# First batch of a fused attention and MLP kernel: residual rows transposed by TensorE in f32, scaled on the way out of PSUM; pieces of work placed between the score products; the last output tile in parts

## The chip, the cores and the metric

The kernel runs on one core of one Trainium2 chip. A core has a matrix engine (TensorE, "PE"; its loads of stationary operands are listed apart as "PEld"), a vector engine (VectorE, "DVE"), a scalar engine (ScalarE, "ACT"), a general engine (GpSimd, "POOL") and a queue engine (SyncE, "SP"). DMA transfers are issued from the queues of SP, ACT and POOL and carried by 16 DMA engines. Each engine works through its own list of instructions in the order of the program and waits at an instruction until what it needs is there. The metric is device time in microseconds (us), as the median of several runs.

## The reference

Eight batches of 384 tokens go through grouped-query attention (16 query heads, 4 key and value heads, head size 64) and then through a residual MLP with affine layers of width 1024 and a hidden size of 4096:

```python
scores = scale * np.matmul(q, k.transpose(0, 1, 3, 2))
attn = softmax(scores)
x = np.matmul(attn, v)                      # B, S, H*D = 8, 384, 1024

a1 = alpha1 * x + beta1
tok = np.einsum('ts,bsd->btd', w_tok, a1)
u = x + lam * tok
a2 = alpha2 * u + beta2
ch = np.maximum(a2 @ w_ch1, 0.0) @ w_ch2
out = u + lam * ch
```

(The softmax is written out in the reference; the two lines are shortened here.) The vectors alpha1, beta1, alpha2, beta2 and lam have one entry for each of the 1024 columns. Inputs and output are f32.

## The kernel before, in words

**Two kinds of work.** `main(b)` is the channel part of batch b: 32 tiles of the hidden layer (`h`, L394, eight matmuls each over the eight 128-column groups of `a2T`), each moved out of PSUM by ACT or DVE (L402, L404) into `hT`; then six output tiles `ch` of 128 x 512 (L418, 32 matmuls each), which DVE scales by lam and adds to the residual (L423, L424) and SP writes out (L425). `side(b)` is everything ahead of that for a batch: transposed q and k, scores, exponentials, attention output, token mixing, and the transposed `a2T`. `side(b + 1)` is cut into units, and while `main(b)` issues its matmuls a loop strews the units between them at an even pace. So for batches 1 to 7 the side work lies inside the main loop of the batch before. Only `side(0)` has no main loop to lie in. It runs alone, ahead of everything, and is called the head in this text.

**The head.** Its order is written out by hand. `scores(i)`, i = 0 to 17, makes one tile of 128 x 1024 scores (L202) and ACT takes its exponential (L211); two PSUM buffers hold score tiles. The dictionary `at` says which other pieces follow which score tile. They are:

- `q_transpose`, `k_transpose`: six transposes on PE into PSUM and one copy out (L189, L179).
- `split`: DVE splits rows of vectors (each f32 row into three bf16 rows) in a chain of casts and subtractions (L498 to L505). The result stands in `rows_b`. For beta1 it also fills `H` in eight instructions (L507).
- `spread`: four matmuls (L311) and one copy (L313) lay a vector out on all 128 partitions in `vecs`.
- `wtok_transpose` (three times, copies at L292) and `rows_r` (L299, then L302 and L303 make `R`): the transposed token weights and their row sums.
- `av_piece(p, 0)` and `(p, 1)`, p = 0 to 7: 18 matmuls (L236) for one pair of heads; then three DVE steps: reciprocal (L241), normalised into the residual tile `x` (L242), and times alpha1 times lam into `a1` (L246), which reads `x` and `vecs`.
- `tok(p)`: 12 matmuls (L258, L262), which need `a1`, `R` and `H`; DVE adds the result to `x` (L265) and then makes `a2` as bf16, `x` times alpha2 (L270).
- `a2_transpose(p)`: for p = 0 to 2 a transposing DMA from SP (L274); for p = 3 to 7 three PE transposes of the bf16 tile (L280) and a copy by ACT (L283).
- `h_part`: the first four `h` tiles (L150) group by group, so that they can begin before all eight groups of `a2T` are there. These 32 matmuls end the head.

PSUM is shared by tag: `sc` and `mm` have two buffers, `tp` and `av` one each. A piece that takes `tp` or `av` waits until the one before it on that tag has been copied out.

**The queues.** POOL casts and places v, k and three quarters of q for batch 0 (L513, L478, L98), and its queue issues all weight loads: chunks of `w_ch1` (L126, 512 KB each as bf16, a ring of five buffers, refilled when `main` is done with a chunk) and `w_ch2` (L131; 2 MB of it in the head, the rest in pieces between the chunks). The dictionary `loads` gives places in the list of units of `side(0)` at which batch 1's k, q and v are asked for. `load_q(1)` waits until batch 0's last `q_transpose` has read the buffer.

**In batch 1's units** (`b == 1`), `split` and four `spread` calls lay out the two vectors that the head did not (beta1 times lam, and lam).

Of the kernel before, what the change touches and what calls it, by code (L numbers as in the profile page):

```python
# [12 lines left out]
def kernel(  # L13
# [54 lines left out]
    w2 = const.tile([P, NNT, DM], bf, tag="w2", name="w2")  # L68
    hT = const.tile([P, NNT, S], bf, tag="hT", name="hT")
    vecs = const.tile([P, 4, DM], f32, tag="vecs", name="vecs")  # L70
    g1, al2, h1, lam_t = (vecs[:, i] for i in range(4))
    bias1 = const.tile([P, NNT], f32, tag="bias1", name="bias1")
    a2Ts = [const.tile([P, NDT, S + 16 * (1 - i)], bf, tag=f"a2T{i}", name=f"a2T{i}") for i in range(2)]
    kT = const.tile([P, NST, Hkv, P], bf, tag="kT", name="kT")
# [81 lines left out]
    def side(b):  # L156
# [96 lines left out]
        def tok(p):  # L253
            tag, n = ("mm", 2) if first else ("av", 1) if pe_flip else ("tp", 1)
            ps = psum.tile([P, NST, P], f32, tag=tag, name="tok", bufs=n)
            for tt in range(NST):
                for st in range(NST):
                    nc.tensor.matmul(out=ps[:, tt, :], lhsT=wtokT[:, st, tt * P:(tt + 1) * P],  # L258
                                     rhs=a1s[p][:, st, :], start=(st == 0),
                                     stop=(st == NST - 1 and not first))  # L260
                if first:
                    nc.tensor.matmul(out=ps[:, tt, :], lhsT=R[:, tt * P:(tt + 1) * P],  # L262
                                     rhs=H[:, cols(p)], start=False, stop=True)
            u = x[:, :, cols(p)]
            nc.vector.tensor_tensor(out=u, in0=ps, in1=u, op=ADD)  # L265
            if first:
                a2s[p] = hTf[:, 7296 + p % 5 * S:7296 + (p % 5 + 1) * S].rearrange("p (a d) -> p a d", a=NST)
            else:
                a2s[p] = sb.tile([P, NST, P], bf, tag="a2", name="a2", bufs=3)
            nc.vector.tensor_tensor(out=a2s[p], in0=u, in1=bc(al2, p), op=MUL)  # L270

        def a2_transpose(p):
            if not pe_flip or first and p < NP - 5:
                nc.sync.dma_start_transpose(  # L274
                    out=a2T[:, p, :S].rearrange("p (a s) -> p a s", a=NST),
                    in_=a2s[p].rearrange("p a d -> p (a d)"))
                return
            ps = tp_ps([P, NST, P], "av" if first and p % 2 else "tp")
            for tt in range(NST):
                nc.tensor.matmul(out=ps[:, tt, :], lhsT=a2s[p][:, tt, :], rhs=ident,  # L280
                                 is_transpose=True, start=(tt == 0), stop=(tt == NST - 1),
                                 skip_group_check=True)
            nc.scalar.copy(out=a2T[:, p, :S], in_=ps.rearrange("p a b -> p (a b)"))  # L283
# [19 lines left out]
            nc.vector.scalar_tensor_tensor(out=R[:32], in0=t, scalar=masks[2], in1=ps[:32], op0=MUL, op1=ADD)  # L303


        def spread(ps_, vs, tag, eng="ACT"):
            n = len(ps_)
            ps = psum.tile([P, 4, P], f32, tag=tag, name="vec", bufs=1)
            w = vs[1] - vs[0]
            for i, p in enumerate(ps_):  # L310
                nc.tensor.matmul(out=ps[:, i * w:(i + 1) * w], lhsT=sel[:, p:p + 1].to_broadcast([P, P]),  # L311
                                 rhs=rows_b[:, vs[0] * P:vs[1] * P], start=True, stop=True)
            evac(eng)(out=vecs[:, vs[0]:vs[1], ps_[0] * P:(ps_[-1] + 1) * P].rearrange("p v (n d) -> p n v d", n=n),  # L313
                      in_=ps[:, :n * w].rearrange("p (n v) d -> p n v d", n=n))
# [10 lines left out]
        if not first:  # L325
            if pe_flip:
                add(k_transpose, 0)
                add(q_transpose, 0, 2, "DVE", "av")
                add(k_transpose, 2)
                add(q_transpose, 2, 2, "DVE", "av")  # L330
                if b == 1:
                    add(split, 3, 4)
            for j in range(NP + 4):
                if 1 < j < NP + 2:
                    add(av_piece, j - 2, 0)
# [8 lines left out]
                    add(a2_transpose, j - 4)  # L344
                if b == 1 and j < 2:
                    for p in (4 * j, 4 * j + 2):
                        add(spread, (p, p + 1), (2, 4), "tp")
                elif j < 2:
                    us.extend([lambda: None] * 2)
            return us  # L350
# [1 line left out]
        add(q_transpose, 0, 1, "DVE", "av")  # L352
        add(q_transpose, 1, 1, "DVE", "tp")
        lower, upper = range(NP // 2), range(NP // 2, NP)
        at = {1: [(warmup, 3), (split, 0, 1)], 2: [(warmup, 2)],
              3: [(q_transpose, 2, 2, "DVE", "av"), (spread, lower, (0, 1), "tp"), (split, 1, 3)],
              4: [(wtok_transpose, 0, "av"), (spread, lower, (1, 2), "tp")],
              5: [(wtok_transpose, 1, "av"), (wtok_transpose, 2, "tp"), (rows_r, "av")],
              7: [(q_transpose, 4, 2, "ACT")], 8: [(k_transpose, 2, "ACT"), (spread, upper, (0, 1), "av")],
              10: [(q_transpose, 6, 2, "ACT")], 12: [(spread, upper, (1, 2), "av")]}  # L360
        for i in range(18):
            add(scores, i)
            for f, *a in at.get(i, []):
                add(f, *a)
            for p in range(NP):
                last = (9 * p + 8) // 4
                if i == last + 1:
                    add(av_piece, p, 0)
                    add(av_piece, p, 1)
                if i == last + 4:  # L370
                    add(tok_flip if p < NP - 5 else tok, p)
        add(av_piece, NP - 1, 0)
        add(av_piece, NP - 1, 1)
        for f, *a in ((a2_transpose, 3), (tok, 6), (a2_transpose, 4), (h_part, (0, 1), range(3)), (tok, 7),
                      (a2_transpose, 5), (h_part, (2, 3), range(3)), (h_part, range(4), (3, 4)), (a2_transpose, 6),
                      (h_part, range(4), (5,)), (a2_transpose, 7), (h_part, range(4), (6,)), (h_part, range(4), (7,))):
            add(f, *a)
        return us

# [3 lines left out]
    def main(b):  # L383
# [29 lines left out]
        for dw in range(NDW):  # L413
            cs = slice(dw * 512, (dw + 1) * 512)
            for ms in range(NST):
                ps = psum.tile([P, 512], f32, tag="mm", name="ch", bufs=2)
                for nt in range(NNT):
                    nc.tensor.matmul(out=ps, lhsT=hT[:, nt, ms * P:(ms + 1) * P],  # L418
                                     rhs=w2[:, nt, cs], start=(nt == 0), stop=(nt == NNT - 1))
                    if nt % 4 == 3 and nt < NNT - 1:  # L420
                        yield T_C
                o = sb.tile([P, 512], f32, tag="tmp", name="o", bufs=4)
                nc.vector.tensor_tensor(out=o, in0=ps, in1=lam_t[:, cs], op=MUL)  # L423
                nc.vector.tensor_tensor(out=o, in0=o, in1=x[:, ms, cs], op=ADD)  # L424
                nc.sync.dma_start(out=out[b].rearrange("(p st) d -> p st d", st=NST)[:, ms, cs], in_=o)  # L425
                yield T_C

    t_all = 2 * NNT * T_H + 8 * NST * NDW * T_C
# [2 lines left out]
    with tc.manual_schedule(engines=order):  # L431
# [16 lines left out]
        qst, vst = (stage[:, i:i + Hkv * NST * D].rearrange("p (h st d) -> p h st d", h=Hkv, st=NST)  # L448
                    for i in (0, Hkv * NST * D))
        wtok_in = stage[:, 1536:2112].bitcast(bf).rearrange("p (tt s) -> p tt s", tt=NST)  # L450
        be2 = stage[:, 2112:2112 + NDT]
        R = stage[:, 2120:2312].bitcast(bf)
        H = stage[:, 2312:2824].bitcast(bf)
        ones = stage[:, 2824:2840].bitcast(bf)
        masks = [stage[:32, 2840 + i:2841 + i] for i in range(3)]
        sel4 = stage[:32, 2844:2852]
        sel = stage[:, 2852:2856].bitcast(bf)
        for t in (stage[:, 2120:2824], rows_b, sel):
            nc.vector.memset(t, 0.0)
        nc.sync.dma_start(out=vst, in_=v[0].rearrange("h (p st) d -> p h st d", st=NST))  # L460

        for i, ap in enumerate((moe_alpha1, moe_alpha2, moe_beta1, moe_lam)):
            nc.sync.dma_start(out=rows_f[:, i * P:(i + 1) * P],
                              in_=bass.AP(tensor=ap.tensor, offset=ap.offset, ap=[[0, 4], [P, NP], [1, P]]))
        load_k(0, [2])
        with nc.allow_non_contiguous_dma(reason="one small vector, once"):
            nc.sync.dma_start(out=be2, in_=moe_beta2.rearrange("(dt di) -> di dt", di=P))
        for h in (0, 2):
            nc.scalar.dma_start(out=qst[:, h:h + 2], in_=q[0, h:h + 2].rearrange("h (p st) d -> p h st d", st=NST))
        xs[0] = sb.tile([P, NST, DM], f32, tag="x", name="x", bufs=2)  # L470
# [12 lines left out]
        for t in vt:  # L483
            nc.vector.memset(t[:, :, :, D:], 1.0)
        AX = mybir.AxisListType.X
        for i, m in enumerate(masks):
            nc.vector.tensor_reduce(out=m, in_=ident[:32, 8 * (i + 1):24 + 8 * (i // 2)], op=ADD, axis=AX)
        nc.vector.tensor_scalar(out=masks[2], in0=masks[2], scalar1=-1.0, scalar2=None, op0=MUL)
# [1 line left out]
            for t, n in ((sel, 24), (sel4, 32)):  # L490
                nc.vector.tensor_reduce(out=t[:n], in_=ident[:n, :n].rearrange("p (k c) -> p c k", c=NP), op=ADD, axis=AX)

        def split(lo, hi):
            c = slice(lo * P, hi * P)
            for i in (0, 2):
                if lo <= i < hi:
                    r = rows_f[:, i * P:(i + 1) * P]
                    nc.vector.tensor_tensor(out=r, in0=r, in1=rows_f[:, 3 * P:], op=MUL)  # L498
            src, dst = rows_f, rows_t
            for m in masks[:2]:  # L500
                nc.vector.tensor_copy(out=rows_b[:32, c], in_=src[:, c])
                nc.vector.scalar_tensor_tensor(out=dst[:, c], in0=rows_b[:32, c], scalar=m, in1=src[:, c],
                                               op0=MUL, op1=mybir.AluOpType.subtract)
                src, dst = dst, src
            nc.vector.tensor_copy(out=rows_b[:32, c], in_=src[:, c])  # L505
            for p in range(NP if lo <= 2 < hi else 0):
                nc.vector.tensor_scalar(out=H[:32, p * P:(p + 1) * P], in0=rows_b[:32, 2 * P:3 * P],  # L507
                                        scalar1=sel4[:, p:p + 1], scalar2=None, op0=MUL)

        place_k(0, 0)  # L510
        for h, cp in ((0, nc.vector.tensor_copy), (2, nc.scalar.copy)):
# [81 lines left out]
```

## Time and profile before

| | |
|---|---|
| median of 9 runs | 819.62 us (818.81 to 820.61) |
| time of the profiled execution | 820.61 us |
| span of its profile | 818.7 us |
| PE busy, share of the span | 797.3 us, 97% |
| DVE, ACT, POOL busy | 352.7, 225.9, 184.5 us |
| first matmul of `main(0)` (L394) | 47.75 us |
| last DVE step of the last output tile | ends at 815.70 us |

The profiled execution is the slowest of the nine, 1.0 us over their median. All positions in the text are us from the start of its span. A row of the timeline gives start, duration, engine, line, operation, the tiles written and read, and in brackets how long the engine had been idle before it and what ended the wait. A matmul's duration holds the time that it takes to run through the array, so a row of matmuls that follow each other closely overlaps the next row; the time that one costs PE is read from start to start.

The head in stretches, busy us of each engine and the mean granted clock of PE:

| stretch | PE | DVE | ACT | POOL | clock |
|---|---|---|---|---|---|
| 6 to 10 | 2.81 | 2.88 | 3.01 | 3.58 | 1.00 |
| 10 to 14 | 1.86 | 3.76 | 2.88 | 4.00 | 1.00 |
| 14 to 18 | 1.15 | 3.96 | 1.15 | 4.00 | 0.72 |
| 18 to 22 | 2.05 | 2.38 | 0.42 | 0.17 | 0.50 |
| 22 to 26 | 4.00 | 3.24 | 1.48 | 0.00 | 0.50 |
| 26 to 30 | 3.51 | 2.59 | 3.94 | 0.00 | 1.00 |

### The profile page before, as it was taken

What the parts mean: (1) busy time and instruction counts of PE and PEld (TensorE: products, weight loads), DVE (VectorE), ACT (ScalarE), POOL (GpSimd) and SP (SyncE); (2) the same over time, 40 slices, a digit from 0 to 9 for tenths busy, and PEclk for the clock granted to TensorE, in tenths of its full rate; (3) what the DMA queues carried; (4) which work ended last, traced back from release to release, by engine and by line L of the source; (5) the groups of instructions that cost most, each with busy time, mean ns of one, the idle gap of its engine ahead of it and who ended that gap; (6) DMA issues with size and microseconds to landing.
All of it is one profiled execution on the core that took longest, in us unless ns stands there. A gap on an engine that the chain in (4) does not pass through costs nothing.

```text
span 818.7 us, 13994 instructions
## 1 busy us (share of the span) xinstructions
PE 797.3 (97%) x6020; PEld 447.1 (55%) x6073; DVE 352.7 (43%) x689; ACT 225.9 (28%) x300; POOL 184.5 (23%) x230
## 2 busy tenths in 40 slices
PE   5999999999999999999999999999999999999997
PEld 2665655565555655556555664556545565556543
DVE  7754554254442444334443444524454344442222
ACT  4745321332114321133112331033210432102100
POOL 6234440225002240022401232022500221003000
PEclk8899999999999999999999999999999999999999
DMA  9999999899959991699927999589995998129610
GB/s 167 198 180 200 202 215 171 134 168 174 80 99 180 172 160 46 136 182 170 146 69 136 178 174 103 107 132 176 173 87 99 152 177 125 36 57 193 87 39 38
DMA packets 260589, 112.85 MB, mean 138 GB/s; under 512 B 109744, under 2 KB 254256, under 8 KB 260528
## 3 DMA queue, kind: packets, MB, share of 16 engines
q0 software_dynamic: 197760, 83.28, 90.0%
q1 hardware_dynamic: 62224, 28.30, 14.4%
q8 instruction: 47, 0.77, 0.4%
q10 hardware_dynamic: 544, 0.39, 0.2%
q14 instruction: 14, 0.11, 0.0%
HBM read 170.53 MB, written 12.58 MB: 224 GB/s over the span
## 4 chain that ended last, share of the span: by engine, by line
PE 88%; DVE 2%; issue 1%; ACT 0%; ACTq 0%; DVEq 0%
PE ch L418 40%; PE h L394 37%; PE av L236 4%; PE sc L202 4%; PE tok L258 3%; DVE a1f L249 0%; DVE x L242 0%; DVE a L251 0%; DVE hT L404 0%; PE tp L280 0%; DVE rinv L241 0%; ACT es L211 0%; DVE o L423 0%; DVE o L424 0%; PE tp L186 0%
## 5 line engine op out<-in xcount | busy, mean ns | idle before, releaser
L394 PE MATMUL h<-a2T,w 128*128 128x384 bf16 (+1 forms) x2016 | 349.4, 327 | 1.0 <-ACT hT L402 0.4
L418 PE MATMUL ch<-w,hT 128*128 128x512 bf16 x1483 | 345.6, 380 | 3.4 <-issue 1.0
L394 PEld LDWEIGHTS <-w 128*128 128x128 bf16 x2016 | 189.3, 98 | 125.5 <-issue 9.0
L126 POOL DMA_DIRECT2D w<-in_moe_w_ch_dram x128 | 112.3, 879 | 545.2 <-PE h L394 494.8
L418 PEld LDWEIGHTS <-hT 128*128 128x128 bf16 x1536 | 142.3, 98 | 155.4 <-issue 4.6
L211 ACT ACTIVATE es<-sc 128x1024 bf16<-128x1024 f32 x126 | 123.2, 1021 | 281.9 <-PE sc L202 281.9
L404 DVE TENSOR_SCALAR hT<-h,bias 128x384 bf16<-128x384 f32 x128 | 79.0, 618 | 187.0 <-PE h L394 186.4
L402 ACT ACTIVATE hT<-h,bias 128x384 bf16<-128x384 f32 x128 | 74.2, 580 | 226.0 <-PE h L394 202.3
L423 DVE TENSOR_TENSOR o<-ch,vecs 128x512 f32<-128x512 f32 x48 | 33.0, 688 | 92.7 <-PE ch L418 92.7
L265 DVE TENSOR_TENSOR x<-tok,x 128x384 f32<-128x384 f32 x64 | 35.5, 555 | 77.4 <-PE tok L258 75.8
L236 PEld LDWEIGHTS <-es 128*128 128x128 bf16 x1008 | 45.8, 97 | 21.4 <-ACT es L211 0.9
L236 PE MATMUL av<-v,es 128*128 128x65 bf16 x1008 | 49.2, 193 | 0.8 <-ACT es L211 0.8
L202 PE MATMUL sc<-qT,kT 64*128 64x384 bf16 (+2 forms) x576 | 45.8, 275 | 0.7 <-ACT hT L211 0.3
L258 PEld LDWEIGHTS <-wtokT 128*128 128x128 bf16 x576 | 38.0, 98 | 13.1 <-issue 0.8
L241 DVE RECIPROCAL rinv<-av 128x6 f32<-128x6 f32 x64 | 12.7, 198 | 66.5 <-PE av L236 66.2
L258 PE MATMUL tok<-a,wtokT 128*128 128x128 bf16 x504 | 37.3, 220 | 0.0
L242 DVE TENSOR_TENSOR x<-av,rinv 128x384 f32<-128x384 f32 x64 | 35.7, 558 | 2.3
L202 PEld LDWEIGHTS <-kT 64*128 64x128 bf16 x576 | 20.2, 94 | 28.3 <-issue 23.8
L424 DVE TENSOR_TENSOR o<-o,x 128x512 f32<-128x512 f32 x48 | 34.7, 722 | 1.6
L270 DVE TENSOR_TENSOR a<-x,vecs 128x384 bf16<-128x384 f32 x56 | 31.4, 561 | 1.9
L251 DVE TENSOR_TENSOR a<-a1f,vecs 128x384 bf16<-128x384 f32 x56 | 31.2, 558 | 2.2
L249 DVE TENSOR_TENSOR a1f<-x,vecs 128x384 f32<-128x384 f32 x56 | 31.2, 558 | 1.9
(69 smaller groups left out, 214.5 us busy)
## 6 DMA issues: line engine op xcount, KB each, us to landing
w<-in_moe_w_ch_dram POOLq DMA_DIRECT2D x135, 512.0 KB, 6.7
out_dram<-o SPq DMA_DIRECT2D x48, 256.0 KB, 2.3
q_raw<-in_q_dram POOLq DMA_DIRECT2D x21, 256.0 KB, 7.9
kst<-in_k_dram SPq DMA_DIRECT2D x16, 192.0 KB, 3.4
w<-in_moe_w_ch_dram POOLq DMA_DIRECT2D x10, 256.0 KB, 11.5
w<-in_moe_w_ch_dram POOLq DMA_DIRECT2D x1, 2048.0 KB, 26.0
v<-in_v_dram POOLq DMA_DIRECT2D x21, 64.0 KB, 7.5
a2T<-a SPq DMA_TRANSPOSE x48, 2.4
```

What stands on the lines that cost most here:

```text
L126: nc.gpsimd.dma_start(out=t, in_=w1src[:, :, c * CW * P:(c + 1) * CW * P])
L202: nc.tensor.matmul(out=sc[:, hh, k % 4:k % 4 + n], lhsT=kT[r, sk, 2 * p // G, :], rhs=qT[r, st:st + n, p, :], start=True, stop=True)
L211: nc.scalar.activation(out=e, in_=sc, func=EXP, scale=scale_qk)
L236: nc.tensor.matmul(out=av[:, hh, sq, :], lhsT=ess[k // 4][:, hh, k % 4, :], rhs=vb[:, sk, hk, :], start=(sk == 0), stop=(sk == NST - 1))
L242: nc.vector.tensor_tensor(out=x[:, :, cols(p)].rearrange("p st (h d) -> p h st d", h=2), in0=av[:, :, :, :D], in1=rinv.to_broadcast([P, 2, ...
L258: nc.tensor.matmul(out=ps[:, tt, :], lhsT=wtokT[:, st, tt * P:(tt + 1) * P], rhs=a1s[p][:, st, :], start=(st == 0), stop=(st == NST - 1 an ...
L265: nc.vector.tensor_tensor(out=u, in0=ps, in1=u, op=ADD)
L394: nc.tensor.matmul(out=ps[:, :n], lhsT=w1[:, dt, j * P:(j + 1) * P], rhs=a2T[:, dt, :n], start=(dt == 0), stop=(dt == NDT - 1))
L402: nc.scalar.activation(out=hT[:, nt, :], in_=ps[:, :S], func=RELU, bias=c1)
L404: nc.vector.tensor_scalar(out=hT[:, nt, :], in0=ps[:, :S], scalar1=c1, scalar2=0.0, op0=ADD, op1=mybir.AluOpType.max)
L418: nc.tensor.matmul(out=ps, lhsT=hT[:, nt, ms * P:(ms + 1) * P], rhs=w2[:, nt, cs], start=(nt == 0), stop=(nt == NNT - 1))
L424: nc.vector.tensor_tensor(out=o, in0=o, in1=x[:, ms, cs], op=ADD)
```

## The change

Four things are done.

1. **The residual rows in the head.** `a2` is no longer made in batch 0. `a2_transpose(p)` takes the f32 rows of `x` and transposes them on PE against an f32 identity, `ident_f`, for all eight p; ACT's step out of PSUM multiplies by alpha2, which is now a value per partition (`al2T`, loaded by one more small DMA). The f32 transposes stand in the program as one instruction each, with no load of weights apart.
2. **The vectors.** `vecs` is ordered alpha1, beta1, alpha2, lam. In the head `split` takes the first two rows together, in two steps, and only alpha1 is spread; `fill_h` makes `H` in one instruction instead of eight. Batch 1's units split and spread the other three (six `spread` calls instead of four).
3. **The order of the head.** `at` lists every piece; the rules that placed `av_piece`, `tok` and the transposes by index are gone. DVE, not ACT, copies out q, k and the head's two spreads.
4. **The last output tile** of the last batch is made in columns 0 to 255, 256 to 383 and 384 to 511, each with its own matmuls, DVE steps and output DMA.

The core of the diff:

```diff
-    g1, al2, h1, lam_t = (vecs[:, i] for i in range(4))
+    g1, h1, al2, lam_t = (vecs[:, i] for i in range(4))
...
         def a2_transpose(p):
-            if not pe_flip or first and p < NP - 5:
+            if first:
+                ps = psum.tile([P, NST, P], f32, tag="av" if p % 2 else "tp", name="ut", bufs=1)
+                for tt in range(NST):
+                    nc.tensor.matmul(out=ps[:, tt, :], lhsT=x[:, tt, cols(p)], rhs=ident_f, is_transpose=True,
+                                     start=(tt == 0), stop=(tt == NST - 1), skip_group_check=True)
+                nc.scalar.activation(out=a2T[:, p, :S], in_=ps.rearrange("p a b -> p (a b)"),
+                                     func=mybir.ActivationFunctionType.Copy, scale=al2T[:, p:p + 1])
+                return
+            if not pe_flip:
...
-                    add(split, 3, 4)
+                    add(split, 2, 4)
...
                     for p in (4 * j, 4 * j + 2):
-                        add(spread, (p, p + 1), (2, 4), "tp")
+                        add(spread, (p, p + 1), (1, 3), "tp", "ACT")
+                    add(spread, range(4 * j, 4 * j + 4), (3, 4), "tp", "ACT")
...
+        at = {1: [(warmup, 3), (split, 0, 2, 0)], 2: [(q_transpose, 2, 2, "DVE", "av"), (split, 0, 2, 1)],
+              3: [(spread, lower, (0, 1), "tp"), (wtok_transpose, 0, "av")],
+              4: [(av, 0), (wtok_transpose, 1, "tp"), (wtok_transpose, 2, "av")], 5: [(fill_h,), (rows_r, "tp")],
+              6: [(av, 1), (q_transpose, 4, 2)], 7: [(tok, 0), (k_transpose, 2)],
+              8: [(av, 2), (spread, upper, (0, 1), "av")], 9: [(tok, 1), (ut, 0)], 10: [(av, 3), (ut, 1)],
+              11: [(q_transpose, 6, 2), (tok, 2)], 12: [(tok, 3)], 13: [(av, 4), (ut, 2)], 14: [(ut, 3)],
+              15: [(tok, 4), (av, 5)], 16: [(ut, 4)], 17: [(av, 6), (tok, 5)]}
...
+        for f, *a in ((h_part, (0, 1), range(4)), (av, 7), (ut, 5), (tok, 6),
+                      (h_part, (2, 3), range(4)), (h_part, range(4), (4,)), (ut, 6), (tok, 7),
+                      (h_part, range(4), (5,)), (ut, 7), (h_part, range(4), (6,)), (h_part, range(4), (7,))):
...
+                for lo, hi in ((0, 256), (256, 384), (384, 512)) if last else ((0, 512),):
...
+        def split(lo, hi, step=None):
...
+            if lo == 0 and step != 1:
+                r = rows_f[:, c].rearrange("p (v d) -> p v d", v=2)
+                nc.vector.tensor_tensor(out=r, in0=r, in1=rows_f[:, None, 3 * P:].to_broadcast([32, 2, P]), op=MUL)
...
+        def fill_h():
+            nc.vector.tensor_tensor(out=H[:32].rearrange("p (n d) -> p n d", n=NP),
+                                    in0=rows_b[:32, None, P:2 * P].to_broadcast([32, NP, P]),
+                                    in1=sel4[:, :, None].to_broadcast([32, NP, P]), op=MUL)
```

In `at`, `av` stands for both halves of `av_piece` and `ut` for `a2_transpose`. The first warm-up of nine matmuls and the three after `scores(1)` stay; the two after `scores(2)` are gone. POOL's list of instructions is as before.

## The prediction, made before the changed kernel ran

> **What bounds the kernel now.** First the page's chain of the work that ended last: it is PE from end to end.
>
> ```profile
> PE 88%; DVE 2%; issue 1%; ACT 0%; ACTq 0%; DVEq 0%
> ```
>
> So from main(0) on (47.75 us) only PE work counts, and what the change can win lies in the head and behind the last matmul. Second, the waits of PE in the first 48 us:
>
> ```profile
> PE vec L311 <- DVE hT L505: 4.3, 2, 3.7
> PE tp L289 <- DVE wtokT L292: 2.5, 1, 2.5
> ```
>
> Third, the timeline of DVE, of POOL and of PE around the longer one:
>
> ```profile
> 12.42 0.33 DVE L501 CAST hT<-hT 32x256 bf16<-32x256 f32 x1
> ...
> 13.29 2.85 DVE L505 CAST hT<-hT 32x256 bf16<-32x256 f32 x1
> ```
>
> ```profile
> 13.46 0.88 POOL L478 COPY q_raw<-qh 128x768 bf16<-128x768 bf16 x1
> 14.23 1.01 POOL L98 CAST k<-kst 128x384 bf16<-128x384 f32 x2
> 15.13 0.87 POOL L478 COPY q_raw<-qh 128x768 bf16<-128x768 bf16 x1
> ```
>
> ```profile
> 12.17 0.35 PE L289 MATMUL tp<-ident,stage 128*128 128x128 bf16 x3
> 16.20 0.61 PE L311 MATMUL vec<-hT,stage 128*128 128x128 bf16 x4 [3.69 <-DVE hT L505]
> ```
>
> The same cast takes 0.33 us at 12.42 and 2.85 us at 13.29, while POOL copies from 13.46 to 16.00: DVE was held by POOL. PE waited behind it, and its clock fell. Fourth, the stretches (PE, PEld, DVE, ACT, POOL busy, clock, DMA):
>
> ```profile
> 16.00:18.00 2.00, 1.15 (x8) 0.58 (x9) 1.96 (x10) 1.15 (x2) 2.00 (x3) 0.50 1.26 139
> 24.00:26.00 2.00, 2.00 (x20) 1.40 (x18) 1.34 (x3) 1.09 (x2) 0.00 (x0) 0.50 1.45 195
> 26.00:28.00 2.00, 1.75 (x37) 1.50 (x36) 1.32 (x4) 2.00 (x3) 0.00 (x0) 0.99 1.45 197
> ```
>
> The mean of 0.72 from 14 to 18 puts the fall at 15.8; half clock lasted until 26.0.
>
> **PE's prices**, start to start at full clock: score tile 0.27 us (four matmuls in 0.54 for two tiles), `av` 0.56 (two halves of 0.28), `tok` in the head 0.66 (12 matmuls of 0.055), `h_part` matmul 0.164 (eight in 1.31), four spread matmuls 0.22. Bf16 transposes:
>
> ```profile
> 30.24 0.51 PE L186 MATMUL tp<-ident,q_raw 128*128 128x128 bf16 x6
> 30.59 0.33 PE L258 MATMUL tok<-hT,wtokT 128*128 128x128 bf16 x3
> ```
>
> six in about 0.33, so 0.055 each.
>
> **The f32 transpose** is in no row. Lower end: 0.055, the bf16 one. Upper end: four bf16 passes, each with its own load laid in front of it instead of hidden (PEld shows 0.098 for one): 4 x (0.098 + 0.055) = 0.61. Nearest is the bf16 transpose with twice the bytes (2 x 0.055) and, as the program has no separate load to pull ahead, one load in front: 0.21, which I take. There are 24: 5.0 us, bounds 1.3 and 14.7. They replace 15 bf16 ones (0.85 us) and three transposing DMAs.
>
> The Trainium skill, TensorE: Matmul & The Clock Gate, sections LDWEIGHTS and Weight-path perf modes, gives a load of 128 columns without the fast path, which f32 lacks, about 107 ns. No row here shows it. With a move of 53 ns that estimate makes 0.16 each, 1.2 us less in all.
>
> **The head, first part.** I lay the new order on the old durations. Up to 9.5 us nothing differs that PE waits for. DVE: the product of two rows with lam starts at 7.7 and is held by POOL's copy until 8.8 (as L498 was, 0.98 against 0.27); cast 0.54, subtraction 0.47, copy of q 0.54, then cast 0.33, subtraction 0.47, cast 0.40: `rows_b` is ready at 11.8. That is before POOL's run at 13.46, so the stall of 3.7 us goes. PE idles from 9.6 to 11.8; then spread 0.22, one w_tok transposition 0.17, `scores(4)` 0.27, `av(0)` 0.56, two w_tok transpositions 0.34, `scores(5)` 0.27: until 13.7.
>
> Where the stall goes: `av(0)` now ends inside POOL's run. Reciprocal 0.20 and L242 0.56 (operand in PSUM) bring DVE to 14.1; L246 reads two SBUF tiles, as L498 did, and I let it be held until 16.15 (1.5 us; nothing if it isn't). Behind it in DVE's list wait two copies of w_tok (0.70) and `fill_h` (32 x 1024; 0.155 us fixed and 1.04 ns per column, from the 384 columns in 0.556 and 512 in 0.69: 1.22), then L302 and L303 (0.55, 0.60). PE waits for the w_tok copies until 16.9 (3.2 us), does `rows_r` 0.48, `scores(6)` and `av(1)`, and waits for `R` to free `tp` until 19.3.
>
> **The clock.** Before, PE was idle from 12.55 to 16.20 and the clock fell at 15.8, 3.25 us after PE had stopped; the idle of 1.04 us ahead of 6.80 left it alone. My gap is over after 3.2 us. Bounds: no loss, or half clock from 15.8 to 26.0 again, in which PE has some 6.6 us of this work and 2.5 us of waits to put against it: 2.5 us later. By the nearest row it is close; I take no loss, narrowly, and keep the other as a rival.
>
> The Trainium skill, same page, The HAM clock gate, says that the clock falls after one idle window of about 3.4 us and that the windows run free. The fall at 15.8 and the rise at 26.0 fit windows of 3.4. By it 3.2 us is just too short to fill one.
>
> **The head, second part**, from 19.3 at full clock: two `q_transpose` 0.66, 11 score tiles 2.97, eight `tok` 5.28, `k_transpose` 0.33, six `av` 3.36, one spread 0.22, 32 `h_part` 5.25: 18.1; the f32 transposes 5.0; waits 1.2 (0.7 where `k_transpose` needs `tp`, which DVE frees only behind `av(1)`'s three steps; 0.2 at `ut(1)`; 0.3 at `ut(7)`, whose cover is four `h_part` of 0.65 against 0.56 for L265 before it and 0.5 for ACT behind it). End: 43.6. ACT has, from `scores(7)` on, 11 exponentials of 1.02 and five scaled copies of about 0.5, 13.7 us in the 14 us until PE needs the last; it is nearly a second bound, so I add what ACT and hand-overs cost the old order beyond the same kind of sum (laid out likewise the old head ends at 47.4, not 47.75) and a little more: 44.25. **The head gains 3.5 us.** Per 0.1 us in the f32 transpose it changes by 2.4.
>
> DVE and ACT, off PE's path: DVE loses eight L270 (4.5 us) and eight L507 (2.0), and gains the copies of q, k and two spreads (2.8) and `fill_h`; ACT loses those and four spreads and gains three copies. SP loses three transposing DMAs (it sat 7.65 us on their issue, with nothing behind them until 45) and gets one small one, which moves beta2's load back by 0.5 us; its values are needed at 24, some 18 us later. POOL's list is unchanged; `load_q(1)` is freed 4 us earlier, but its bytes stand behind the 2 MB of weights that land at 43 either way.
>
> **main(0).** Two more spreads: eight matmuls of 0.055, 0.4 us on PE; DVE's wider split is 0.6 longer, ACT gets two copies of 0.58. These are covered by the PE work between units; uncovered, they could cost another 0.6. The weights set a limit: the chunk for the last two `h` tiles, issued at 79.28, lands 12.2 us later, at 91.5, and is used at 93.06, so 1.6 us of slack. But DMA ran dry at 50 to 52 us (146 GB/s, around it 200), because the first refills (47.90) waited for the head's end. With the head 3.5 us earlier they stand behind batch 1's q and v without a gap, some 2 to 3 us earlier. Slack plus gap, about 4 to 4.5, covers 3.5.
>
> **The last tile.** Before:
>
> ```profile
> 814.28 0.69 DVE L423 TENSOR_TENSOR o<-ch,vecs 128x512 f32<-128x512 f32 x1 [5.49 <-PE ch L418]
> 815.01 0.69 DVE L424 TENSOR_TENSOR o<-o,x 128x512 f32<-128x512 f32 x1
> ```
>
> Now two steps of 128 columns, 0.29 each, end the chain: 0.61 in place of 1.41, 0.8 less. PE: 32 x (0.109 + 0.055 + 0.055) = 7.0 against 32 x 0.216 = 6.9, 0.1 more. The last output's packets moved for about 0.9 us; a quarter of it 0.2 to 0.4: 0.5 less, bounds 0 and 0.7. Together 1.2 less, bounds 0.7 and 1.4.
>
> **Sum**, against the profiled execution: 820.61 - 3.5 + 0.4 - 1.2 = 816.3 us. That execution lies 1.0 above its median, so 3.3 below the median of 819.62. Within 0.2% (1.64 us; about what this kernel's measurement can tell from no change) is 817.98 to 821.26.
>
> **Rivals.**
>
> - *The f32 transpose costs several passes.* For: no row excludes it, and PE is the bound from 19.3 on, so nothing hides it. Against: it is a move of data only. From 0.28 the win is under 0.2%; it decides from 0.42 on (816.3 + 24 x 0.21 = 821.3): slower. At 0.45: 822.1; at 0.61: 825.9. Chance 0.17, of which 0.14 slower and 0.03 no change.
> - *Half clock again.* For: the gap is only 0.45 us shorter than the one that let the clock fall. Against: it ends before the fall came. 816.3 + 2.5 = 818.8, no change. Chance 0.18, 0.05 of it still faster, where less work falls into the slow stretch.
> - *The weights arrive no earlier.* For: DMA is near 200 GB/s through the whole stretch. Against: the dry spell at 50. Gain capped at 1.6: 820.61 - 1.6 - 1.2 = 817.8, just faster. Chance 0.06.
> - *New waits in the order* (a copy of q or k on DVE late behind `av`, ACT the bound): 3 us or more lost, 819 to 822. Chance 0.07: 0.05 slower, 0.02 no change.
>
> The forecast has 0.52. Faster 0.52 + 0.06 + 0.05 = 0.63, no change 0.03 + 0.13 + 0.02 = 0.18, slower 0.14 + 0.05 = 0.19. Range: best, the bf16 price (end 41.6 + 0.4, capped by the weights at 4.5) and the best tail: 820.61 - 4.5 + 0.4 - 1.4 = 815.1, with a full microsecond more if DVE isn't held and the weights come sooner still, 814.0; upper end 822.0, the transpose at 0.45. The forecast's own range is 814.5 to 818.
>
> **What would show it.** `main(0)` starts near 44.2; f32 transposes start to start near 0.21; the clock stays 1.00 after the warm-up; L246 of p = 0 takes about 2 us beside POOL's copies; PE idles 3 us before `rows_r`; no PE wait for weights near 85; the last DVE step ends about 0.65 us after the last matmul, not 1.45. Wrong, if the transposes are above 0.3, the clock falls, or PE waits in the second part exceed 2 us.

## The result and the profile after

The changed kernel takes 815.70 us (median of 11 runs, 814.98 to 818.72) against 819.61 of the kernel before beside it (33 runs, 818.22 to 820.61): a ratio of 0.9958, 95% interval 0.9950 to 0.9967. Predicted were 816.3. The profiled execution happens to be the slowest of the eleven (818.72, span 816.9). A second profile of the same kernel is nearer the usual case and is read below beside the first: its execution took 816.43 (span 814.7), the slowest of its own five, whose median is 815.66.

Both spans are cut at two marks: the first matmul of `main(0)`, and DVE's first step on the last tile but one. Between them lies the main part, behind them the tail.

| | before | after, first profile | after, second profile | predicted for after |
|---|---|---|---|---|
| head, until `main(0)` starts | 47.75 | 42.08 | 43.50 | 44.25 |
| main part | 759.63 | 763.35 | 759.72 | +0.4 |
| tail, until the span ends | 11.32 | 11.47 | 11.48 | -1.2 |
| span | 818.7 | 816.9 | 814.7 | -4.3 |

Signed numbers in the last column are changes against the first. So the second profile's execution won 4.25 in the head, lost 0.1 in the main part and 0.15 in the tail: 4.0 in all. Now the lines behind the cells, first profile unless said otherwise. The page's head, its clock row and its chain of the work that ended last:

```profile
span 816.9 us, 14117 instructions
...
PEclk9999999999999999999999999999999999999999
...
PE 92%; DVE 4%; DMA 3%; issue 1%; POOL 0%; ACT 0%; ACTq 0%; DVEq 0%
```

PE still sets the end, but DMA is new in the chain with 3%. PE's waits up to 46 us (us in total, times, longest):

```profile
PE tp L186 <- DVE stage L310: 1.4, 1, 1.4
PE r L306 <- DVE wtokT L299: 1.4, 1, 1.4
PE vec L318 <- DVE hT L517: 1.3, 1, 1.3
```

The waits of 3.7 and 2.5 us of before are gone; three of 1.3 to 1.4 stand in their place, where the prediction named them (2.2, 3.2 and 1.1 there, in the order of the program). Why the second is shorter, DVE's timeline shows:

```profile
14.31 0.90 DVE L246 TENSOR_TENSOR hT<-x,vecs 128x384 bf16<-128x384 f32 x1
15.13 0.61 DVE L299 COPY wtokT<-tp 128x384 bf16<-128x384 bf16 x2
15.66 1.75 DVE L521 TENSOR_TENSOR stage<-hT,stage 32x1024 bf16<-32x1024 bf16 x1
```

and POOL's beside it:

```profile
15.52 0.82 POOL L488 COPY q_raw<-qh 128x768 bf16<-128x768 bf16 x1
16.30 1.20 POOL L538 CAST a2T<-stage 128x8 bf16<-128x8 f32 x1
```

L246 took 0.34 us more than undisturbed (0.90 against 0.56), not 1.5 more, and now a step of POOL is longer too: its cast of 128x8 takes 1.20 us beside DVE's L521, and 0.55 in the second profile.

The f32 transposes, as a tile's instructions (duration min/median/max in ns, first and last start):

```profile
L275 PEld LDWEIGHTS ut<-hT,x x24: 137/140/144, 22.9 to 40.4; 128*128 128x128 f32 x24
L275 PE MATMUL ut<-hT,x x24: 273/273/330, 23.0 to 40.5; 128*128 128x128 f32 x24
L277 ACT ACTIVATE a2T<-ut,stage x8: 575/580/584, 23.5 to 40.8; 128x384 bf16<-128x384 f32 x8
```

and PE's timeline, which gives them start to start:

```profile
24.35 0.55 PE L275 MATMUL ut<-hT,x 128*128 128x128 f32 x3
24.83 0.39 PE L202 MATMUL sc<-qT,kT 64*128 64x128 bf16 x4
...
38.40 0.49 PE L275 MATMUL ut<-hT,x 128*128 128x128 f32 x3
38.73 0.33 PE L258 MATMUL tok<-hT,wtokT 128*128 128x128 bf16 x3
```

Three take 0.48 us ahead of a score tile and 0.33 ahead of `tok`. The rows around score tiles are longer for other work too: a lone `tok` matmul ahead of one takes 0.15 (26.12 to 26.27), where 0.055 is its price. So a transpose costs 0.11 from one to the next, and the eight groups of three, each from its start to the start of the next piece, take 3.4 us together, 0.14 each. The 273 ns are latency, not rate. The profile also lists a load for every transpose, although the program has one instruction for both; three loads of 0.14 alone would take 0.42, so the loads overlap with what runs before them.

Now the beginning of the main part, PE's timeline:

```profile
42.08 1.47 PE L399 MATMUL h<-a2T,w 128*128 128x385 bf16 x8
...
47.89 0.61 PE L186 MATMUL tp<-ident,q_raw 128*128 128x128 bf16 x4 [2.58 <-DMA q_raw<-in_q_dram]
48.28 2.75 PE L399 MATMUL h<-a2T,w 128*128 128x385 bf16 x8
```

and the stretches around it (PE, PEld, DVE, ACT, POOL busy, clock, DMA share, GB/s):

```profile
46.00:48.00 2.00, 0.11 (x2) 0.12 (x3) 0.47 (x1) 0.00 (x0) 1.07 (x2) 0.86 1.54 213
48.00:50.00 2.00, 2.00 (x10) 1.14 (x10) 0.56 (x1) 0.00 (x0) 0.00 (x0) 0.50 1.48 196
```

PE waits 2.58 us for batch 1's q, with nothing else to do from 46 to 48, and the clock falls behind it: eight `h` matmuls take 2.75 instead of 1.47. Together these (2.58 and 1.28) account for the 3.7 us by which this main part is longer.

Last, the tail. PE's timeline, then DVE's:

```profile
809.40 1.95 PE L426 MATMUL ch<-w,hT 128*128 128x128 bf16 x32 [0.52 <-DVE o L431]
811.73 1.95 PE L426 MATMUL ch<-w,hT 128*128 128x128 bf16 x32 [0.38 <-DVE o L431]
```

```profile
805.43 0.69 DVE L431 TENSOR_TENSOR o<-ch,vecs 128x512 f32<-128x512 f32 x1 [5.49 <-PE ch L426]
...
813.72 0.29 DVE L431 TENSOR_TENSOR o<-ch,vecs 128x128 f32<-128x128 f32 x1 [1.71 <-PE ch L426]
814.04 0.29 DVE L432 TENSOR_TENSOR o<-o,x 128x128 f32<-128x128 f32 x1
```

The last steps are as short as forecast, but PE now waits for DVE before parts two and three: all three parts lie in one PSUM buffer, and the next part's first matmul starts only when DVE has read the part before.

### The profile page after: what moved, and what is told of

The parts are those of the page before. It is cut to its first block, busy times and chain, and to the rows that moved or that the text cites. A ratio compares the mean times of both kernels' runs of the same rounds, so it can differ in the third digit from the quotient of the medians.

```text
span 816.9 us, 14117 instructions
## 1 busy us (share of the span) xinstructions
PE 798.5 (98%) x6090; PEld 450.8 (55%) x6144; DVE 347.4 (43%) x678; ACT 225.1 (28%) x298; POOL 186.1 (23%) x230
## 4 chain that ended last, share of the span: by engine, by line
PE 92%; DVE 4%; DMA 3%; issue 1%; POOL 0%; ACT 0%; ACTq 0%; DVEq 0%
PE ch L426 41%; PE h L399 39%; PE av L236 4%; PE sc L202 4%; PE tok L258 4%; DMA q_raw<-in_q_dram 2%; DVE x L242 1%; DMA stage<-in_q_dram 1%; DVE hT L409 1%; DVE a1f L249 0%; DVE a L251 0%; PE tp L186 0%; POOL q_raw L108 0%; PE vec L318 0%; DVE hT L246 0%
## 5 line engine op out<-in xcount | busy, mean ns | idle before, releaser
L426 PE MATMUL ch<-w,hT 128*128 128x512 bf16 (+2 forms) x1546 | 346.1, 371 | 4.4 <-issue 1.0
L426 PEld LDWEIGHTS <-hT 128*128 128x128 bf16 x1600 | 145.9, 98 | 153.1 <-issue 5.8
L431 DVE TENSOR_TENSOR o<-ch,vecs 128x512 f32<-128x512 f32 (+2 forms) x50 | 33.3, 667 | 91.1 <-PE ch L426 91.1
L432 DVE TENSOR_TENSOR o<-o,x 128x512 f32<-128x512 f32 (+2 forms) x50 | 33.6, 671 | 1.7
```

What stands on the lines that cost most here:

```text
L426: nc.tensor.matmul(out=ps[:, lo:hi], lhsT=hT[:, nt, ms * P:(ms + 1) * P], rhs=w2[:, nt, dw * 512 + lo:dw * 512 + hi], start=(nt == 0), sto ...
L432: nc.vector.tensor_tensor(out=o[:, lo:hi], in0=o[:, lo:hi], in1=x[:, ms, c], op=ADD)
```

## The experiments

### The last tile undivided

```diff
-                for lo, hi in ((0, 256), (256, 384), (384, 512)) if last else ((0, 512),):
+                for lo, hi in ((0, 512),):
```

> The changed kernel with the last output tile undivided, as before. Theory (tail parts give nothing, because the second and third part's matmuls wait until DVE has read the part before them out of the same PSUM buffer, 0.52 and 0.38 us in the changed kernel's trace): the time from the first DVE step of the last tile but one to the end of the span is 11.3 us again (11.5 with parts), and the time is 0 to 0.3 us below the changed kernel's. Rival (the prediction's sum, parts worth 1.2): 0.9 to 1.3 us above it.

Measured: 816.16 us (815.34 to 816.41, 5 runs), ratio 0.9960 [0.9946, 0.9974]. The tail is 11.51 us in the trace, against 11.47 and 11.48 in parts, so the parts won nothing, as the theory has it. The median, 0.46 above the changed kernel, fits neither number well; the runs of the two overlap.

### An own PSUM buffer for each part

```diff
                 for lo, hi in ((0, 256), (256, 384), (384, 512)) if last else ((0, 512),):
+                    if lo:
+                        ps = psum.tile([P, 512], f32, tag="mm", name="ch", bufs=2)
```

> The changed kernel with a PSUM buffer of its own for each part of the last tile. Theory (the waits come from the shared PSUM buffer): no PE wait between the parts, the last DVE step ends 8.0 us after the first DVE step of the last tile but one instead of 8.9, time 0.8 to 1.0 us below the changed kernel's. Rival (the parts wait for something else, or narrow matmuls are slower in themselves): waits stay, time within 0.3 us of the changed kernel's.

Measured: **814.60 us** (814.26 to 815.26, 5 runs), ratio 0.9945 [0.9932, 0.9957], the best of this study. PE's timeline of the end is one unbroken group:

```profile
799.64 10.68 PE L428 MATMUL ch<-w,hT 128*128 128x512 bf16 x111
```

and DVE's:

```profile
803.29 0.69 DVE L433 TENSOR_TENSOR o<-ch,vecs 128x512 f32<-128x512 f32 x1 [5.49 <-PE ch L428]
...
810.69 0.29 DVE L434 TENSOR_TENSOR o<-o,x 128x128 f32<-128x128 f32 x1
```

From the first of these to the span's end (813.5) it is 10.21 us: 1.26 less than with one buffer, and 1.11 less than the 11.32 of the kernel before. The waits came from the shared buffer, as the theory has it.

### Batch 1's q ahead of half of the weights

```diff
-        loads = {9: [(load_w1, RING - 1), (load_w2, 0, 0, 2)], 20: [(late_loads,)], 30: [(load_q, 1)], 37: [(load_v, 1)]}
+        loads = {9: [(load_w1, RING - 1), (load_w2, 0, 0, 4)], 20: [(late_loads,)], 30: [(load_q, 1)],
+                 37: [(load_v, 1), (load_w2, 0, 1, 4)]}
```

> The changed kernel with the second megabyte of the 2 MB weight load issued behind batch 1's q and v instead of ahead of them. Theory (main(0) stands still for 2.6 us at 45.3 because batch 1's q is queued behind those weights, and PE's clock may fall in that gap): q has landed before it is needed, no PE wait for q_raw, clock 1.00 from 42 to 54, time 2.3 to 3.0 us below the changed kernel's median and no run near 818. Rival (the DMA engines are the bound of the whole stretch, so a later wait for weights takes its place): under 1 us gained, PE waits for w or on the copies behind it.

Measured: 815.94 us (815.25 to 817.06, 5 runs), ratio 0.9962 [0.9949, 0.9975]. PE's waits from 44 to 110 us:

```profile
PE h L399 <- ACT hT L407: 0.9, 2, 0.5
PE h L399 <- DVE bias L405: 0.3, 1, 0.3
PE h L399 <- DMA w<-in_moe_w_ch_dram: 0.2, 1, 0.2
```

The wait for q is gone, yet the median isn't better. The theory, which took the first profile's 2.58 us for the rule, fell. The rival's number (under 1 us gained) fits, though the wait for w that it names is only 0.2 us. The wait for q had been 0.65 in the undivided kernel's profile and 1.72 in that with own buffers; what it is as a rule is taken up in the last experiment.

### Casts to bf16 on DVE, in place of f32 transposes

```diff
             if first:
+                a2s[p] = hTf[:, 7296 + p % 5 * S:7296 + (p % 5 + 1) * S].rearrange("p (a d) -> p a d", a=NST)
+                nc.vector.tensor_copy(out=a2s[p], in_=u)
                 return
...
-                    nc.tensor.matmul(out=ps[:, tt, :], lhsT=x[:, tt, cols(p)], rhs=ident_f, is_transpose=True,
+                    nc.tensor.matmul(out=ps[:, tt, :], lhsT=a2s[p][:, tt, :], rhs=ident, is_transpose=True,
```

> The changed kernel with DVE casting the residual rows to bf16 (eight more DVE casts of 128 x 384) and bf16 transposes; the scale by alpha2 stays on ACT's way out of PSUM. Theory (the head is no longer what sets the time; batch 1's q is): the transposes cost 0.055 instead of 0.155 each, PE work in the head 2.4 us less, main(0) starts 1 to 2 us earlier, the wait for q grows by the same, time within 0.5 us of the changed kernel's. Rival (head time carries through): 1 to 2 us below it. Rival 2 (DVE's eight casts make it late): main(0) starts no earlier or later.

Measured: 816.96 us (816.00 to 817.46, 7 runs), ratio 0.9970 [0.9959, 0.9981], 1.3 above the changed kernel; `main(0)` starts at 43.25. The waits of PE up to 46 us that the other profiles don't have:

```profile
PE tp L277 <- DVE hT L268: 1.6, 3, 0.7
...
PE tok L258 <- DVE hT L246: 0.5, 1, 0.5
```

The transposes are cheaper on PE (the eight groups take 1.9 us instead of 3.4; the expectation's 0.155 each was read from the groups ahead of score tiles), but they wait for the casts: the rival in which DVE's casts come late was right. The fair comparison for `main(0)` is the first profile's 42.08, the only other one of the changed head without half clock: 1.17 later. What the f32 path is worth is not PE's time but that DVE has eight steps less in a head where PE waits for DVE.

### The kernel before, profiled a second time

> The kernel before, unchanged, for a second look at its head. Theory (the kernel before's spread of 818 to 821 us comes from whether PE's clock falls in its head): if this execution is near 820.5 the clock fell as in the first profile and main(0) starts near 47.7; if near 818.5 to 819.5 it did not fall, or fell for a shorter time, and main(0) starts 1 to 2 us earlier. Rival (the spread has another source): main(0) starts within 0.3 us of 47.75 whatever the time.

Measured: one run, 820.08 us, span 818.2; `main(0)` at 47.22, main part 759.61, tail 11.37. PE's wait for the cast at L505 is smaller, 2.7 us, and the half clock lies elsewhere (7.7 to 11.1 and 14.5 to 24.8 us, read from stretches of 1 us). The head of before moves by half a microsecond between executions; its other two parts by 0.05. The rival, which allowed 0.3, falls. Whether the clock makes the spread is not tested: it fell here too, for longer in all, and at 820.08 the execution is not one of the short ones (818.4 to 819.5) that the theory speaks of.

### Keeping PE warm in the kernel before

```diff
-              4: [(wtok_transpose, 0, "av"), (spread, lower, (1, 2), "tp")],
+              4: [(wtok_transpose, 0, "av"), (warmup, 18), (spread, lower, (1, 2), "tp")],
```

The added matmuls compute nothing that is used.

> The kernel before with 18 idle-time warm-up matmuls (2.9 us) in the gap after 12.5 us; they compute nothing that is used. Theory (of the 3.9 us that the change won, at most a part is the clock: the head with half clock from 15.8 to 26.0 costs about 2 us): clock 1.00 throughout the head, main(0) starts 1.5 to 2.5 us before 47.75, median 0.5 to 1.5 us below the kernel before's, upper group of times near 820.5 gone. Rival (the waits on DVE hide the slow clock, as three runs of changed kernels suggest, where the clock fell and main(0) still started at 42.3 to 42.6): under 0.5 us.

Measured: 824.43 us (824.03 to 825.07, 5 runs), ratio 1.0058 [1.0045, 1.0070], and a miss as an experiment. PE's waits up to 48 us:

```profile
PE warm L436 <- DVE wtokT L292: 6.7, 1, 6.7
```

The matmuls that were to fill the gap read `wtokT`, and the copy into it just ahead of them (L292) ended only at 19.23, behind all that DVE had before it. So PE stood still for longer, the clock fell all the same (16.9 to 23.7 us), and the added matmuls came on top. It says nothing about what the clock alone is worth.

### The early split alone, in the kernel before

```diff
-        at = {1: [(warmup, 3), (split, 0, 1)], 2: [(warmup, 2)],
-              3: [(q_transpose, 2, 2, "DVE", "av"), (spread, lower, (0, 1), "tp"), (split, 1, 3)],
+        at = {1: [(warmup, 3), (split, 0, 3)], 2: [(warmup, 2)],
+              3: [(q_transpose, 2, 2, "DVE", "av"), (spread, lower, (0, 1), "tp"), (fill_h,)],
```

`fill_h` is here the old code's eight instructions for `H`, taken out of `split`.

> The kernel before with all three rows split in one go after score tile 1, and H filled after the first spread, in the same place as the second split was. Everything else, the old order and the bf16 transposes included, stays. Theory (the 3.7 us stall behind the cast that POOL holds is the largest single loss of the old head): no wait of PE near 12.5 to 16, but L246 or the fill of H is held by POOL instead, main(0) starts 1 to 2 us earlier, time 1 to 2 us below the kernel before's. Rival (the order dealt out evenly, not the split, is what gains): under 0.5 us.

Measured: 818.26 us (817.23 to 820.39, 11 runs), ratio 0.9986 [0.9977, 0.9995]; `main(0)` at 44.97, main part 759.90, tail 11.33. PE's waits up to 48 us:

```profile
PE tp L289 <- DVE wtokT L292: 3.3, 1, 3.3
...
PE vec L311 <- DVE hT L505: 1.2, 1, 1.2
```

The stall behind the cast falls to 1.2 us, and the wait for the copies of `w_tok` grows from 2.5 to 3.3: it moves on to the next DVE steps beside POOL's copies. So the theory's time is right and its "no wait of PE near 12.5 to 16" is not. PE waits for batch 1's q here too, 0.57 us at 48.76. The median wins 1.1 to 1.5 us, some third of the change's 3.9; the rival, which left the split under 0.5, falls.

### Own buffers, and two pieces of the head exchanged

```diff
-              4: [(av, 0), (wtok_transpose, 1, "tp"), (wtok_transpose, 2, "av")], 5: [(fill_h,), (rows_r, "tp")],
-              6: [(av, 1), (q_transpose, 4, 2)], 7: [(tok, 0), (k_transpose, 2)],
+              4: [(av, 0), (wtok_transpose, 1, "tp"), (wtok_transpose, 2, "av")], 5: [(rows_r, "tp"), (fill_h,)],
+              6: [(q_transpose, 4, 2), (av, 1)], 7: [(tok, 0), (k_transpose, 2)],
```

> The changed kernel with a PSUM buffer for each part of the last tile, the row sums ahead of the fill of H, and the third q transposition ahead of av(1). Theory (the 1.4 us wait of PE for R to free its PSUM buffer comes from H ahead of it on DVE): PE's wait for R falls below 0.5 us, main(0) starts 0.5 to 1 us earlier than 42.3, time 0.3 to 1.0 us below that of the changed kernel with PSUM buffers of their own (814.6). Rival (batch 1's q lands at 45 to 48 whatever the head does): the wait for q grows by as much, time unchanged against 814.6.

Measured: 815.29 us (814.05 to 816.13, 5 runs), ratio 0.9943 [0.9930, 0.9957], no better than own buffers alone. PE's wait for `R` is 0.9 us, not below 0.5, and `main(0)` starts later, at 44.07. The stretches:

```profile
18.00:20.00 2.00, 2.00 (x28) 1.51 (x25) 1.69 (x4) 0.00 (x0) 1.21 (x2) 0.50 1.40 189
20.00:22.00 2.00, 2.00 (x20) 1.83 (x18) 1.41 (x3) 1.02 (x1) 0.00 (x0) 0.50 1.31 220
```

Here half clock (17.1 to 23.9 us) met a PE with work all the time, and nothing to put against it. Neither theory nor rival had reckoned with that; the order itself stays undecided.

### Own buffers and q first together, and the changed kernel a second time

The first of these carries both diffs from above, the second none.

> Both edits together: an own PSUM buffer for each part of the last tile, and batch 1's q loaded ahead of the second half of the weights. Theory (the tail's 1.26 us is the only gain; PE's wait for q, 0.65 to 2.6 us in the other profiles, mostly lies on top of the wait for ACT's hT and is worth at most half a microsecond): median 814.1 to 814.8, no wait of PE for q between 44 and 52 us, main(0) starts at 42.0 to 42.7, and from the first DVE step of the last-but-one tile to the span's end 10.2 us. Rival (the wait for q is paid in full, some 1.7 us as in the profile with own buffers): median 812.6 to 813.4.

> The changed kernel unchanged, a second profile. Theory (its first profile caught an unusually long wait for q, 2.58 us, and the half clock behind it): the wait for q is 0.5 to 1.9 us, from the start of main(0) to the first DVE step of the last-but-one tile 760 to 761.3 us instead of 763.35, median 815.5 to 816.2. Rival (the 2.58 us belong to this kernel in every execution): wait 2.3 or more, 763 us or more, and the head of 42.1 us is then what makes the time.

Measured, both edits: 815.00 us (813.94 to 815.67, 5 runs), ratio 0.9943 [0.9931, 0.9956]; no wait for q, tail 10.17 us. The median is 0.2 above the theory's interval and 1.6 above the rival's, so the wait for q doesn't look paid in full. The comparison isn't clean, for the start of `main(0)` was missed: 43.31. Its head had the long hold that the prediction had reckoned with, in DVE's timeline

```profile
14.44 2.11 DVE L246 TENSOR_TENSOR hT<-x,vecs 128x384 bf16<-128x384 f32 x1
```

and in PE's waits up to 46 us:

```profile
PE r L306 <- DVE wtokT L299: 2.6, 1, 2.6
```

Measured, the changed kernel again: 815.66 us (815.32 to 816.43, 5 runs), ratio 0.9951 [0.9937, 0.9964]. PE's timeline at the place where the first profile has the wait for q:

```profile
43.50 1.47 PE L399 MATMUL h<-a2T,w 128*128 128x385 bf16 x8
...
46.45 0.50 PE L186 MATMUL tp<-ident,q_raw 128*128 128x128 bf16 x6
47.37 1.47 PE L399 MATMUL h<-a2T,w 128*128 128x385 bf16 x8 [0.42 <-ACT hT L407]
```

No wait for q at all, so the 2.58 us are not this kernel's rule, and the rival falls; the theory's 0.5 to 1.9 was too high as well. Put together, over the six profiles with this order of the head (waits from each one's own timeline):

| kernel | `main(0)` starts | PE waits for q | sum | main part without that wait |
|---|---|---|---|---|
| changed, first profile | 42.08 | 2.58 | 44.66 | 760.77 |
| own buffers | 42.26 | 1.72 | 43.98 | 759.31 |
| undivided | 42.63 | 0.65 | 43.28 | 759.61 |
| changed, second profile | 43.50 | 0 | 43.50 | 759.72 |
| q first | 42.34 | 0 | 42.34 | 760.10 |
| own buffers, q first | 43.31 | 0 | 43.31 | 759.72 |

Where the loads are in the change's order, the sooner the head ends, the longer PE waits for q; with a head of 43.5 it doesn't wait. What the head gains beyond about 43.3 is given back there, and in the first profile half clock took 1.3 more. It is not only that q is needed sooner: the last part of q landed at 47.9, 47.2, 46.4 and 46.2 us in the first four rows, latest where it had been asked for first. Why it lands later is open. That the transfers cause it is shown for the wait itself, not for the time: the loads in another order take the wait away, but the medians (815.94 against 815.70; 815.00 against 814.60) show no gain from it.

## Why the prediction was right, and where two errors met

The sign and nearly the size were right (816.3 against 815.70). In the second profile's execution the sum -3.5 + 0.4 - 1.2 = -4.3 stands beside -4.25 + 0.1 + 0.15 = -4.0: the head won more than was said, the tail nothing. That the totals lie so close is luck in this respect: a head gain put too low and a tail gain put too high nearly cancel. In the first profile's execution they don't (-5.67 + 3.72 + 0.15 = -1.8).

**The f32 transpose** was mis-sized: 0.21 us taken, 0.11 measured from one to the next and 0.14 with what lies at the ends of a group, within the bounds 0.055 to 0.61. The step that failed is the load laid in front of each: the profile lists a load for each, but it overlaps. What is left of the term, twice the bf16 price, is the measured 0.11. Over 24 it is 3.4 us instead of 5.0, 1.6 less. From the start of `q_transpose` behind `rows_r` to `main(0)` the first profile has 42.08 - 18.57 = 23.51 against 24.95 of the prediction, 1.44 less; so the rest of this part took some 0.2 more than reckoned, and the runs don't say where. The estimate of 0.16 from the Trainium skill, TensorE: Matmul & The Clock Gate, section LDWEIGHTS, adds a move to a load of 107 ns; as a rate it is too high as well, since the measured 0.11 has no room for both one after the other. The load's record lasts 140 here. The rival of several passes, which decides from 0.42 on, is out.

**The head's first part** was right in its mechanism. The early split ends the stall of 3.7 us (alone it brings `main(0)` forward by 2.3 to 2.8, against the two profiles of before), and what is late next is the step that was named, L246 beside POOL's copies, and behind it the copies of `w_tok`. The size is not a constant: in the six profiles of the table above L246 took 0.56 to 2.11 us (0.90 and 1.08 in the changed kernel's two), and PE's wait for the copies behind it 0.6 to 2.6, where 2.06 and 3.2 were said. `q_transpose` began at 18.57 and 19.37 in the two profiles of the changed kernel; forecast was 19.3.

**The clock.** "No loss, narrowly" held in the first profile and in that with the casts, and in none of the others of the changed head. The second profile's stretches:

```profile
8.00:10.00 2.00, 1.98 (x15) 0.86 (x14) 1.65 (x3) 2.00 (x3) 2.00 (x3) 0.50 0.83 75
...
18.00:20.00 2.00, 2.00 (x28) 1.55 (x24) 1.57 (x5) 1.02 (x1) 0.50 (x1) 0.50 1.32 184
20.00:22.00 2.00, 2.00 (x23) 1.47 (x22) 1.45 (x4) 1.02 (x1) 0.00 (x0) 0.61 1.36 219
```

So the premise, that a gap must reach some 3.25 us, was wrong: in six of the eight profiles of the changed head the clock fell, which the prediction names as a sign of being wrong. That the first profile lost nothing in its head was luck. What half clock costs depends on where it lies. Where it ended by 19.4 us (own buffers, undivided, q first), `main(0)` began at 42.26 to 42.63, against 42.08 without it. In the second profile, with 13.7 us of it until 21.6, `q_transpose` began 0.80 later and the work from there to `main(0)` took 24.13 instead of 23.51, 0.62 more; up to there PE also waits for DVE. With the two exchanged pieces it lay where PE was full, and `main(0)` began at 44.07, though there the order differs too. The rival's price of 2.5 us, for half clock from 15.8 to 26.0, is neither confirmed nor refuted: no run of the changed head had it there.

**main(0).** The two more spreads and the wider split cost 0.1 (759.72 against 759.63), not 0.4. No wait for the weights of the last `h` tiles appears. The step that failed is that on `load_q(1)`: the prediction says that its bytes "stand behind the 2 MB of weights that land at 43 either way", and didn't go on to what needs them. The weights landed at 41.3 and 40.7 in the changed kernel's two profiles, q's last part at 47.9 and 46.2. An earlier `main(0)` needs q just as much earlier, and the waiting time of 0 to 2.6 us was left out of the sum.

**The last tile** is the step with a wrong mechanism. The terms -0.8, +0.1 and -0.5 took PE as going on without a break from part to part. With one PSUM buffer it can't: 0.52 and 0.38 us of waits, and the first DVE step of the first and the second part comes onto the path. With own buffers the tail is 1.11 us shorter than before, where 1.2 had been said: the terms were nearly right for a kernel that this change isn't.

**Not separated** are the rest of the order, `fill_h` in one instruction, the copies moved from ACT to DVE and the three removed DMA transposes; none of them was tried alone. The early split's 1.1 to 1.5 us (in the kernel before) and the casts' 1.3 (in the changed one) are what single edits showed of the 3.9; for the rest of it the profiles show only that it lies in the head.

## What to carry to other kernels

If a tile is cut into parts so that its end overlaps, ask which buffer each part lives in: here the parts of one PSUM buffer ran one after the other, with the reader in between. When a stage is made to end sooner, go through everything that the next stage needs first, the transfers above all, and see whether each comes sooner as well. And where an engine ahead of PE is the short one, moving work from it to PE can pay, though PE's own sum grows.

## What was not expected of the hardware

**The clock falls after short gaps too.** Read from stretches of 1 us, it was half from 7.9 to 21.6 us (changed, second profile), 12.5 to 19.4 (own buffers), 12.4 to 19.2 (undivided), 11.7 to 15.1 (q first), 17.1 to 23.9 (two pieces exchanged) and 16.7 to 20.1 (own buffers, q first): 13.7, 6.8, 6.8, 3.4, 6.8 and 3.4 us, all near multiples of 3.4. The fall at 7.9 followed a single wait of 1.39 us, which ended at 6.85, and one of 0.20; that at 11.7 came 1.9 us into a wait of 2.05. The first profile, with waits of 0.98 and 1.34, has no fall in its head. The Trainium skill, TensorE: Matmul & The Clock Gate, The HAM clock gate, speaks of one idle window of about 3.4 us, free-running. The length and the free running agree with these runs; that the window must be idle throughout does not, since in the 3.4 us ahead of those two falls PE was at work for some 1.8 and 1.3 us. Part of that work was transposes; which work keeps the clock up, and how much of it, no run here shows.

**Steps of DVE and POOL that run beside each other can take longer, on either side and differently in each execution.** The same 128x384 step on DVE took 0.56, 0.90, 1.08 and 2.11 us, and the same 128x8 cast on POOL 1.20 and 0.55 in the two profiles of one kernel. Where the DVE step took 0.56 beside POOL (own buffers), POOL's next copy took 1.81 instead of 0.83. That one engine holds the other is read from these overlaps; no run takes the work of either away.
